# Top-k attention and two MoE layers on one core: keys and queries turned as plain numbers, scores of two heads on two halves of the array's rows, weight conversion without a drain

## The chip, the cores and the metric

The kernel runs on one core of a Trainium2 chip. Its time is the device time of one execution in microseconds; the kernel before took 2362.32 us, the median of three runs.

## The reference

Three stages follow each other. The inputs are 32-bit floats.

```python
# attention: 4 batches, 8 heads, 576 rows, head size 64
scores = scale * np.matmul(q, k.transpose(0, 1, 3, 2))
kth = np.partition(scores, -32, axis=-1)[..., -32:-31]
scores = np.where(scores >= kth, scores, -1e9)
attn = softmax(scores)                  # with 1e-9 added to the sum
x = matmul(attn, v)                     # as [2304 tokens, 512]
# first MoE: no nonlinearity, so w3 @ w_out is one matrix W
x = ((x @ w1) * (x @ w2)) @ w3 @ w_out  # 512 -> 1024 -> 512
# second MoE: 8 experts, gate by 8 rounds of row and column sums
P = exp(x @ w_gate - max); P = sinkhorn(P, 8)
out = sum(P[:, e:e+1] * (relu(x @ w1[e]) @ w2[e]) for e in range(8))
```

## The kernel before

**Numbers in two parts.** Where precision is wanted at the rate of one pass, a 32-bit number is split into a part that the array's rounded format (float32r) holds, hi, and the rest, lo. A product of two such numbers is the sum of three or four products of parts. Plain 32-bit products run on TensorE as two instructions each.

**Attention.** The 32 heads come as 16 visits, a visit being a pair of heads of one batch. The work is 72 steps: a step takes 128 query rows of both heads of a visit, and every ninth step takes the last 64 rows of two visits together. A step is a pipeline of operations with one-letter names: S0 and S1 (st_scores, the scores of head 0 and of head 1 of the next step, on TensorE, then a copy out by ScalarE and a sum of halves by GpSimd), T0 and T1 (st_top, a maximum of the score halves on VectorE), f, d, g, e (finding and dropping the eight largest of 288 numbers, VectorE, ten of them), V and J (tail and join, L299 to L306), O (st_over), E (st_exp), N, R and A (normalising, turning and multiplying the weights of the two steps before by the values). The letters F, P, C and X are where other work is put: F runs some of `fill`, P a piece of the preparation of keys and queries, C one tick of the weight conversion (convert), X takes up a finished batch. The strings in ORDERS are that order, written out by hand: one for the first ten steps, one for the rest.

**Keys and queries.** load_pair brings a visit's keys and queries. prep_split splits them in their natural layout (ScalarE rounds, GpSimd subtracts); hi and lo of one head stand side by side, 128 wide. prep_group turns nine blocks each of keys and of queries on TensorE, so hi stands on rows 0 to 63 and lo on rows 64 to 127, and ScalarE evicts them. prep_swap makes by DMA a second copy of the keys with hi and lo exchanged. A score is then two products over all 128 rows: one with the plain copy and one with the swapped copy.

**Weights.** w_out (8 tiles), w3 (16), w1 (8) and w2 (8) pass through a conversion of three ScalarE operations, one on VectorE (c1, L458) and one or two on GpSimd (cv_run, run_cv); c1 is put three slots ahead in dve_q, which every find and drop advances by one. From w3 and w_out the matrix W is made on TensorE, in `fill`, 5500 ns of it a step. NCA is the number of conversions before those of w2. When it is reached, run_cv waits until nothing is under way, frees the space of w3 and w_out (wt_close), opens that of w2 and begins again. When all is converted, moe1_pool opens the pool of the first MoE, at the earliest in step 19 (marks[0]).

**First MoE.** moe1_list gives the work of a batch in two parts of 256 and 320 tokens: ab makes the two products (12 instructions for each block of 128 outputs), x2_mm the product with W, logits the gate's products. `per` spreads the work of batches 0 to 2 evenly over the steps up to the last mark; batch 3 follows the attention. Then the second MoE runs, which the change doesn't touch.

Of the kernel before, what the change touches and what calls it, by code (L numbers as in the profile page):

```python
# [7 lines left out]
F32 = mybir.dt.float32  # L8
# [10 lines left out]
def kernel(  # L19
# [14 lines left out]
    nc = tc.nc  # L34
# [28 lines left out]
    wg = const.tile([128, KD, E], F32, name="wg")  # L63
    nc.sync.dma_start(wg, w_gate.rearrange("(c p) e -> p c e", p=128))
# [17 lines left out]
    nc.vector.tensor_scalar(ident, jp, 0.0, None, op0=ALU.is_equal)  # L82
    nc.gpsimd.memset(zf, 0.0)
# [12 lines left out]
    nat = {}  # L96
    tx = aps.tile([128, 1024], F32, name="tx")
    vn_t = [ap1.tile([128, 2 * R + 2, D], F32, name=f"vn{i}") for i in range(2)]
    qst_t = [ap1.tile([128, 2 * S4 + 256], F32R, name=f"qst{i}") for i in range(2)]
    for i in range(2):  # L100
        nc.gpsimd.memset(vn_t[i][:, 2 * R:, :], 0.0)
        nc.gpsimd.tensor_copy(qst_t[i][:, 2 * S4 + 64:2 * S4 + 192], zf)

    def load_pair(p):
        b, hp, (t0, t1), tail = visits[p]
        for nm, src, r0, r1, end in (("k", k, 0, R, True), ("q", q, t0, t1, tail)):
            t = ap1.tile([128, 2 * R + 1, D], F32, name=f"{nm}n", tag=f"{nm}n", bufs=1)
            nc.sync.dma_start(
                t[:, 0:2 * R].rearrange("p (h r) d -> p h (r d)", h=2)[:, :, D * r0:D * r1],
                src[b, 2 * hp:2 * hp + 2, 0:S4, :].rearrange("h (p r) d -> p h (r d)", r=R)[:, :, D * r0:D * r1])  # L110
            for i in range(2 if end else 0):
                nc.sync.dma_start(t[64 * i:64 * i + 64, 2 * R], src[b, 2 * hp + i, S4:S, :])
            nat[nm, p] = t
# [11 lines left out]
    split = {}  # L125
# [7 lines left out]
    def prep_split(p, nm, eng=nc.gpsimd):  # L133
        src = nat.pop((nm, p))
        hl = ap1.tile([128, 2 * R + 1, 2, D], F32R, name=f"{nm}hl", tag=f"{nm}hl")
        (t0, t1), tail = visits[p][2:]
        if nm == "k" or t1 - t0 == R:
            parts = [(src, hl[:, :, 0, :], hl[:, :, 1, :])]
        else:
            hr = hl[:, 0:2 * R].rearrange("p (h r) a d -> p h r a d", h=2)[:, :, t0:t1]  # L140
            parts = [(src[:, 0:2 * R].rearrange("p (h r) d -> p h r d", h=2)[:, :, t0:t1], hr[:, :, :, 0], hr[:, :, :, 1])]
            if tail:
                parts.append((src[:, 2 * R], hl[:, 2 * R, 0], hl[:, 2 * R, 1]))
# [3 lines left out]
        split[nm, p] = hl  # L147

    def qgroups(p):
        (t0, t1), tail = visits[p][2:]  # L150
        n = t1 - t0
# [1020 lines left out]
```

## Time and profile before

| what | value |
| --- | --- |
| median of 3 runs | 2362.32 us (2360.91 to 2363.93) |
| profiled execution | 2362.73 us, span 2360.9 us |
| TensorE (PE) busy | 2262.7 us, 96% |
| VectorE (DVE) busy | 1880.0 us, 80% |
| ScalarE (ACT) busy | 1260.2 us, 53% |
| GpSimd (POOL) busy | 1569.1 us, 66% |
| last join of the attention | 729.8 us |
| chain of work that ended last | 85% TensorE, 6% VectorE, 3% ScalarE, 3% GpSimd |

The span is the time from the first to the last instruction in the trace; the time of the same execution is 1.8 us longer. The busy shares are means over stages that have different limits. The attention with the conversion of the weights and three quarters of the first MoE takes the first 730 us, the rest of the first MoE about 100, the second MoE the rest.

### The profile page before, as it was taken

To read this page: it belongs to the slowest core of one execution; us is meant where nothing else is said; L and a number is where in the kernel's file an instruction comes from. 1 tells how busy PE (TensorE), PEld (TensorE's weight loads), DVE (VectorE), ACT (ScalarE), POOL (GpSimd) and SP (SyncE) were. 2 spreads that over 40 slices of the span, in tenths; PEclk is the share of its full clock that TensorE was granted. 3 is DMA by queue.
4 is the path that set the end of the run, shared out by engine and by line. 5 is a ranking of instruction groups with operands and counts; after the bars stand their busy time and mean duration, and the time that the engine had idled before them with its cause. 6 is when DMAs were issued, how large, how long until landed. Compare 5 with 4: busy or idle time off the path is not lost.

```text
span 2360.9 us, 39073 instructions
## 1 busy us (share of the span) xinstructions
PE 2262.7 (96%) x13155; PEld 2002.8 (85%) x13155; DVE 1880.0 (80%) x4386; ACT 1260.2 (53%) x2751; POOL 1569.1 (66%) x1726
## 2 busy tenths in 40 slices
PE   4797799999999999999999999999999999999999
PEld 3555699998998988899999988898988999999998
DVE  7999999999994378887778777777777777777776
ACT  6999788788774334443443453344434434344432
POOL 5888876776763156866666687666666666666664
PEclk7898899999999999999999999999999999999999
DMA  5433111111101022222222232222222322222221
GB/s 150 129 120 98 44 51 39 41 45 51 31 21 44 26 72 85 70 69 72 64 71 72 86 94 65 70 64 71 66 69 65 97 72 63 72 63 72 68 68 54
DMA packets 172313, 161.95 MB, mean 69 GB/s; under 512 B 21712, under 2 KB 136400, under 8 KB 172112
## 3 DMA queue, kind: packets, MB, share of 16 engines
q1 hardware_dynamic: 172112, 159.45, 22.7%
q8 instruction: 104, 1.70, 0.3%
q14 instruction: 97, 0.79, 0.1%
HBM read 140.53 MB, written 9.44 MB: 64 GB/s over the span
## 4 chain that ended last, share of the span: by engine, by line
PE 85%; DVE 6%; ACT 3%; POOL 3%; issue 1%; DMA 1%; SPq 0%; POOLq 0%; DVEq 0%; ACTq 0%
PE y L1059 33%; PE l1ps L998 29%; PE abps L582 9%; PE x2ps L600 5%; PE sps L240 3%; PE tx L383 2%; PE tx L349 2%; DVE tkv L289 2%; DVE rest L294 1%; PE pt L164 1%; DVE G L458 1%; PE tx L350 0%; DVE low L294 0%; PE lgps L620 0%; ACT s_sb L330 0%
## 5 line engine op out<-in xcount | busy, mean ns | idle before, releaser
L887 POOL TENSOR_TENSOR wal<-ws,wah 128x256 fp32r<-128x256 f32 x665 | 548.7, 833 | 475.9 <-ACT wah L886 468.3
L1072 DVE SCALAR_TENSOR_TENSOR acc<-y,P,acc 128x512 f32<-128x512 f32 x540 | 402.6, 745 | 206.3 <-PE y L1059 204.4
L886 ACT ACTIVATE wah<-ws 128x256 fp32r<-128x256 f32 x672 | 276.6, 413 | 516.5 <-PE l1ps L998 512.4
L1059 PE MATMUL y<-wbh,hh 128*128 128x512 f32 x1152 | 453.8, 394 | 5.2 <-ACT hh L1019 5.2
L1059 PE MATMUL y<-wbl,hh 128*128 128x512 f32 x1152 | 455.2, 395 | 0.0
L1059 PE MATMUL y<-wbh,hl 128*128 128x512 f32 x1152 | 451.9, 392 | 1.6 <-DVE hl L1022 1.2
L880 DVE TENSOR_TENSOR ws<-ws 128x256 f32<-128x256 f32 x384 | 326.1, 850 | 0.4 <-DMA ws<-in_moe_w_dram 0.3
L998 PE MATMUL l1ps<-xo0h,wah 128*128 128x384 f32 x896 | 302.7, 338 | 0.0
L998 PE MATMUL l1ps<-xo0l,wah 128*128 128x384 f32 x896 | 301.2, 336 | 0.0
L998 PE MATMUL l1ps<-xo0h,wal 128*128 128x384 f32 x896 | 301.0, 336 | 0.0
L1019 ACT ACTIVATE hh<-u 128x384 fp32r<-128x384 f32 x192 | 101.0, 526 | 296.8 <-DVE u L1011 296.8
L1059 PEld LDWEIGHTS y<-wbl,hh 128*128 128x128 f32 x1152 | 216.3, 188 | 49.1
L1059 PEld LDWEIGHTS y<-wbh,hh 128*128 128x128 f32 x1152 | 216.4, 188 | 32.3 <-ACT hh L1019 7.6
L1059 PEld LDWEIGHTS y<-wbh,hl 128*128 128x128 f32 x1152 | 216.6, 188 | 30.3 <-DVE hl L1022 4.9
L895 POOL TENSOR_TENSOR wbl<-ws,wbh 128x1024 fp32r<-128x1024 f32 x96 | 232.2, 2418 | 11.6 <-ACT wbh L894 0.2
L266 POOL TENSOR_TENSOR low<-s_sb 128x288 int32<-128x288 int32 x144 | 118.0, 820 | 98.6 <-ACT s_sb L244 95.0
L998 PEld LDWEIGHTS l1ps<-xo0l,wah 128*128 128x128 f32 x896 | 168.5, 188 | 17.2
L998 PEld LDWEIGHTS l1ps<-xo0h,wah 128*128 128x128 f32 x896 | 168.2, 188 | 14.4
L289 DVE MAX8 tkv<-rest 128x8 f32<-128x288 f32 x432 | 175.0, 446 | 0.0
L998 PEld LDWEIGHTS l1ps<-xo0h,wal 128*128 128x128 f32 x896 | 168.5, 188 | 0.0
L240 PE MATMUL sps<-kst,qst 128*128 128x288 f32 x640 | 133.2, 337 | 36.2 <-DVE top L273 35.0
L1011 DVE TENSOR_TENSOR u<-l1ps,u 128x384 f32<-128x384 f32 x288 | 157.2, 546 | 4.3 <-PE l1ps L998 2.5
(157 smaller groups left out, 5241.0 us busy)
## 6 DMA issues: line engine op xcount, KB each, us to landing
ws<-in_moe_w_dram SPq DMA_DIRECT2D x384, 128.0 KB, 2.3
ws<-in_moe_w_dram SPq DMA_DIRECT2D x96, 512.0 KB, 3.5
raw<-in_moe_w_dram SPq DMA_DIRECT2D x32, 512.0 KB, 3.8
kst<-kst SPq DMA_DIRECT2D x30, 288.0 KB, 4.0
xr<-x2s SPq DMA_DIRECT2D x12, 384.0 KB, 3.7
kn<-in_k_dram SPq DMA_DIRECT2D x16, 256.0 KB, 2.8
qn<-in_q_dram SPq DMA_DIRECT2D x16, 256.0 KB, 2.9
raw<-in_moe_w_out_dram SPq DMA_DIRECT2D x8, 512.0 KB, 4.2
```

The source lines that it names most:

```text
L240: nc.tensor.matmul(ps[:, e, 0:SH], lhs, kst[p, part][:, hh, SH * e:SH * e + SH], start=(n == 0), stop=(n == len(terms) - 1))
L289: nc.vector.max(vt[:, j, c:c + 8], x[:, j])
L582: nc.tensor.matmul(ps[:, 0:n], lhs[:, c, fs], rhs[:, c, 0:n], start=(c == 0 and j == 0), stop=(c == KD - 1 and j == 2))
L600: nc.tensor.matmul(ps[:, 0:n], W[:, f, 128 * c:128 * c + 128], G[:, f, 0:n], start=(f == 0), stop=(f == FC - 1))
L880: nc.vector.tensor_tensor(st[:, dst], st[:, x], st[:, y], op)
L886: nc.scalar.activation(hi, st[:, slot], AF.Copy)
L887: eng.tensor_tensor(lo, st[:, slot], hi.bitcast(F32), ALU.subtract)
L895: nc.gpsimd.tensor_tensor(lo, st, hi.bitcast(F32), ALU.subtract)
L998: nc.tensor.matmul(ps[:, 0:TH], lhs[:, c], rhs[:, slot, c], start=(k_ == 0), stop=(k_ == 3 * KH - 1))
L1011: nc.vector.tensor_tensor(t[nm], ps, t[x], ALU.add)
L1059: nc.tensor.matmul(ps, lhs[:, m, h, o:o + 128], rhs[:, m], start=(k_ == 0), stop=(k_ == 5))
L1072: nc.vector.scalar_tensor_tensor(a, ps, P[:, t, e:e + 1], a, op0=ALU.mult, op1=ALU.add)
```

## The change

- Keys and queries of both heads of a visit are loaded side by side, turned as plain numbers (five blocks each, prep_turn), and split after that (prep_parts). The two heads then stand on rows 0 to 63 and 64 to 127. There is no swapped copy.
- A score is four products of parts over 64 rows. st_scores takes one half of the keys for both heads; products of head 0 and head 1 alternate, on the two halves of the rows, into two banks. In the steps of last rows the two heads of a visit stand in blocks of a 128-row weight.
- st_sum runs after the second half, and st_top is one operation on both heads; T0 is gone.
- The conversion isn't drained before w2: its tiles live in a pool of their own, w2 in eight pairs of tiles over the space of w3 and w_out, opened by convert when W is made; scratch (cb) goes to xT. Waiting times of the conversion are shorter (1 tick for 4, 4 for 6).
- The gate's products of a part are made by gate_parts, four products side by side on 32 columns each, and summed by gate_sums with the constant `fold`.
- The start is reordered, and ORDERS has new strings, the third for steps in which the first MoE runs.

```diff
-    wg = const.tile([128, KD, E], F32, name="wg")
-    nc.sync.dma_start(wg, w_gate.rearrange("(c p) e -> p c e", p=128))
+    wg = const.tile([128, KD, 32], F32, name="wg")
+    nc.gpsimd.memset(wg, 0.0)
+    nc.sync.dma_start(wg[:, :, 0:E], w_gate.rearrange("(c p) e -> p c e", p=128))
+    fold = const.tile([128, 32], F32, name="fold")
...
-            t = ap1.tile([128, 2 * R + 1, D], F32, name=f"{nm}n", tag=f"{nm}n", bufs=1)
...
+            t = ap1.tile([128, R + 1, 2, D], F32, name=f"{nm}n", tag=f"{nm}n", bufs=1)
+            for i in range(2):
+                nc.sync.dma_start(t[:, r0:r1, i], src[b, 2 * hp + i, 0:S4, :].rearrange("(p r) d -> p r d", r=R)[:, r0:r1])
+            if end:
+                nc.sync.dma_start(t[0:SR, R], src[b, 2 * hp:2 * hp + 2, S4:S, :].rearrange("h s d -> s h d"))
...
+    def prep_turn(p, nm):
...
+        rows = src.rearrange("p r h d -> p r (h d)")
+        xt = ap1.tile([128, S], F32, name=f"{nm}t", tag=f"{nm}t", bufs=1)
+        by = scale if nm == "q" else 1.0
+        pt = mps.tile([128, 512], F32, name="pt", tag="mm")
+        for t in range(t0, t1):
+            nc.tensor.transpose(pt[:, 128 * t:128 * t + 128], rows[:, t], ident)
+        copy(xt[:, 128 * t0:128 * t1], pt[:, 128 * t0:128 * t1], None, by)
+        if tail:
+            pt = mps.tile([128, 512], F32, name="pt", tag="mm")
+            nc.tensor.transpose(pt[:, 0:SR], rows[0:SR, R], ident[0:SR, 0:SR])
+            copy(xt[:, S4:S], pt[:, 0:SR], None, by)
+        flat_x[nm, p] = xt
+
+    def prep_parts(p, nm, eng=nc.gpsimd):
+        xt = flat_x.pop((nm, p))
+        (t0, t1), tail = visits[p][2:]
+        if nm == "k":
+            kst[p] = ap1.tile([128, 2, S], F32R, name="kst", tag="kst", bufs=2)
+            parts = [(xt, kst[p][:, 0], kst[p][:, 1])]
         else:
...
+            d = qst_t[p % 2]
+            parts = [(xt[:, 128 * t0:128 * t1], d[:, 0, 128 * t0:128 * t1], d[:, 1, 128 * t0:128 * t1])]
+            for i in range(2 if tail else 0):
+                r, c = slice(64 * i, 64 * i + 64), slice(S4 + 64 * i, S4 + 64 * i + 64)
+                parts.append((xt[r, S4:S], d[r, 0, c], d[r, 1, c]))
         for x, hi, lo in parts:
             nc.scalar.activation(hi, x, AF.Copy)
             eng.tensor_tensor(lo, x, hi.bitcast(F32), ALU.subtract)
...
+    def st_scores(st, e):
         ps = aps.tile([128, 2, 512], F32, name="sps", tag="sps")
...
+        cols = slice(SH * e, SH * e + SH)
+        parts = [(a, c) for a in range(2) for c in range(2)]
+        for n, (a, c) in enumerate(parts):
+            for j in range(2):
+                p, h, t = steps1[st][j]
+                if h is None:
+                    lhs, rhs = qst_t[p % 2][:, a, S4:S4 + 128], kst[p][:, c, cols]
+                else:
+                    rows = slice(64 * h, 64 * h + 64)
+                    lhs, rhs = qst_t[p % 2][rows, a, 128 * t:128 * t + 128], kst[p][rows, c, cols]
+                nc.tensor.matmul(ps[:, j, 0:SH], lhs, rhs, start=(n == 0), stop=(n == len(parts) - 1))
...
+        nc.scalar.activation(s_sb[st][:, :, cols], ps[:, :, 0:SH], AF.Copy)
+        if e:
+            sps[st] = ps
+            st_sum(st)
...
+    def st_top(st):
+
+        top_sb[st] = ap1.tile([128, 2, SH], F32, name="top", tag="top", bufs=2)
+        nc.vector.tensor_tensor(top_sb[st], sps.pop(st)[:, :, 0:SH], s_sb[st][:, :, 0:SH], ALU.max)
...
-        cb = cv["p"].tile([128, CW], F32, name="cb", tag="cb", bufs=2)
+        cb = xT[1][:, HP - 2 + n, 0:CW]
...
-                cv_post.append((tick[0], split))
+                cv_post.append((tick[0], split, pos))
...
-                lambda: later(6, w_items(i, hf)))
+                lambda: later(4, w_items(i, hf)))
...
     def wt_close():
-        cvx.close()
         wt.close()
...
+        for c in reversed(range(KD)):
+            for hf in reversed(range(2)):
+                m1p["w2"][c, hf] = [pool.tile([128, CW], F32R, name=f"{n}{2 * c + hf}") for n in ("w2h", "w2l")]
...
+    def gate_parts(b, hf):
+        n = hf[1] - hf[0]
+        st = [x2t.pop((b, hf, c)) for c in range(KD)]
+        ps = mps.tile([128, 512], F32, name="lgps", tag="mm")
+        for c in range(KD):
+            nc.tensor.matmul(ps[32 * c:32 * c + 32, 0:n], wg[:, c], st[c][:, 0:n], start=True, stop=True,
+                             tile_position=(0, 32 * c))
+        nc.scalar.activation(st[1][:, 0:n], ps[:, 0:n], AF.Copy)
+        x2t[b, hf] = st[1]
+
+    def gate_sums(b, hf):
...
-            nc.tensor.matmul(ps[:, E * i:E * i + E], st[:, 128 * i:128 * i + 128], wg[:, c], start=True, stop=True)
+            nc.tensor.matmul(ps[:, E * i:E * i + E], st[:, 128 * i:128 * i + 128], fold[:, 0:E], start=True, stop=True)
...
+                        if f == 0 and wh + pt == 1 and gates:
+                            r.append(gates.pop(0))
...
-        if n == NCA and "w2" not in m1p:
-            if any(dve_q) or cv_post or fill or later_q or (FC - 1, 1) not in w3done:
-                return
-            wt_close()
-            for i in range(2):
-                cvs[n + i][1]()
-            return
-        if key not in raws or n - 2 in open_c1 or n - (3 if n < NCA else 2) in unsplit:
+        if n - 2 in open_c1 or n - 3 in unsplit:
             return
...
+    load_pair(0)
+    for i in range(RB):
+        cvs[i][1]()
...
+    prep_turn(0, "k")
+    prep_parts(0, "k", nc.vector)
+    prep_turn(0, "q")
+    prep_parts(0, "q", nc.vector)
     load_pair(1)
     load_v(0)
...
     st_scores(0, 0)
-    st_top(0, 0)
+    run_cv()
     st_scores(0, 1)
-    st_top(0, 1)
+    while dve_q:
+        dve_slot()
+    st_top(0)
     run_cv()
     run_cv()
...
     ORDERS = (
...
+        "X C N F f0 O0 S0 d0 P f1 d1 R0 O1 B F R1 f2 d2 f3 L F g0 C C P F P C C E0 F V e0 F E1 Q g1 S1 A C F F J T1",
+        "X P C N C O0 C O1 B f0 S0 C L d0 F f1 d1 F R0 F f2 E0 d2 f3 C E1 Q P g0 R1 C C F F V S1 e0 F g1 C C C T1 C C A F J F",
+        "C X f0 O0 O1 C C C N B L S0 F d0 P f1 F d1 f2 E0 d2 F f3 R0 E1 F C S1 Q F g0 V e0 C R1 F P g1 T1 C C F A J C C C C C",
     )
...
     def convert():
-        while cv_post and cv_post[0][0] <= tick[0] - 4:
+        if "w2" not in m1p and (FC - 1, 1) in w3done and not fill and not later_q:
+            wt_close()
+        while cv_post and cv_post[0][0] <= tick[0] - 1 and (cv_post[0][2] < NCA or "w2" in m1p):
             cv_post.pop(0)[1]()
...
-        order = ORDERS[0 if s < SWITCH else 1].split()
+        order = ORDERS[0 if s < SWITCH else 2 if "p" in m1p else 1].split()
```

## Rows read from the trace of the kernel before

**Rows 1.** Joins at L303: durations in ns, first and last start in us.

```profile
L303 DVE TENSOR_TENSOR tkv<-xm,tkv x72: 169/181/193, 29.5 to 729.8; 128x32 f32<-128x32 f32 x72
...
L303 DVE TENSOR_TENSOR tkv<-xm,tkv x1: 181/181/181, 197.0 to 197.0; 128x32 f32<-128x32 f32 x1
...
L303 DVE TENSOR_TENSOR tkv<-xm,tkv x6: 169/181/185, 185.7 to 239.3; 128x32 f32<-128x32 f32 x6
...
L303 DVE TENSOR_TENSOR tkv<-xm,tkv x1: 181/181/181, 271.2 to 271.2; 128x32 f32<-128x32 f32 x1
...
L303 DVE TENSOR_TENSOR tkv<-xm,tkv x1: 180/180/180, 284.1 to 284.1; 128x32 f32<-128x32 f32 x1
```

**Rows 2.** Stretches: engines' busy us (x instructions), PEclk, DMA share, GB/s.

```profile
130.90:197.00 66.10, 58.58 (x342) 37.29 (x342) 63.88 (x211) 65.24 (x134) 55.22 (x65) 1.00 0.34 103
197.00:274.00 77.00, 52.01 (x360) 41.39 (x358) 74.48 (x254) 68.43 (x142) 70.75 (x84) 0.80 0.28 86
...
420.00:600.00 180.00, 179.53 (x1496) 162.96 (x1495) 172.78 (x651) 143.40 (x319) 127.61 (x184) 1.00 0.16 43
```

**Rows 3.** VectorE's waits, 300 to 740 us: total, times, longest in us.

```profile
DVE top L273 <- ACT s_sb L244: 6.6, 16, 1.0
DVE lg L631 <- PE lgps L625: 4.7, 1, 4.7
DVE tkv L289 <- POOL low L278: 3.3, 7, 0.8
DVE rden L306 <- POOL rden L337: 2.4, 3, 1.1
```

**Rows 4.** Pieces of the chain that ended last: start us, us, what.

```profile
280.99 1.43 PE abps L582 x12
282.42 0.53 PE sps L240 x4
...
287.61 0.44 PE pt L164 x4
...
295.11 1.31 PE tx L371 x40
...
320.91 1.73 PE x2ps L600 x8
...
512.10 1.76 PE abps L582 x12
...
561.60 2.16 PE x2ps L600 x8
```

**Rows 5.** Timeline of TensorE's weight loads: start us, us, instruction, count.

```profile
509.93 0.54 PEld L620 LDWEIGHTS lgps<-wg,x2st 128*128 128x128 f32 x4
510.40 0.19 PEld L582 LDWEIGHTS abps<-xh,w1h 128*128 128x128 f32 x1
```

**Rows 6.** The conversions' VectorE operation at L458: least, median, most ns.

```profile
L458 DVE SCALAR_TENSOR_TENSOR G<-G,cb x40: 732/950/1623, 21.7 to 261.4; 128x512 uint16<-128x512 f32 x40
```

**Rows 7.** Timeline of the start, with idle time before an instruction and its releaser.

```profile
8.12 0.60 ACT L129 ACTIVATE kst<-pt 128x512 fp32r<-128x512 f32 x1 [2.00 <-PE pt L164]
...
16.94 0.50 PE L240 MATMUL sps<-kst,qst 128*128 128x288 f32 x2 [1.05 <-DMA kst<-kst]
```

**Rows 8.** Timeline of TensorE's products in a mixed step.

```profile
507.42 0.31 PE L582 MATMUL abps<-xh,w2l 128*128 128x320 f32 x1
507.66 1.31 PE L383 MATMUL tx<-et,vn 128*64 128x128 f32 x20
508.90 1.32 PE L240 MATMUL sps<-kst,qst 128*128 128x288 f32 x8
510.06 0.51 PE L620 MATMUL lgps<-wg,x2st 128*128 128x8 f32 x4
```

**Rows 9.** Timeline of VectorE in the same stretch: one st_top.

```profile
502.69 0.45 DVE L273 TENSOR_TENSOR top<-sps,s_sb 128x288 f32<-128x288 f32 x1
```

More of the change, by code (lines that the diff above doesn't have):

```diff
@@ L259, with st_sum @@
     low_sb, top_sb, sps, tails = {}, {}, {}, {}
[L261 to L273 removed]
+    def st_sum(st):
+        low_sb[st] = ap1.tile([128, 2, SH], F32, name="low", tag="low", bufs=2)
+        x = s_sb[st].bitcast(I32)
+        for j in range(2):
+            nc.gpsimd.tensor_tensor(low_sb[st][:, j].bitcast(I32), x[:, j, 0:SH], x[:, j, SH:S], ALU.add)
+    def st_top(st):
+        top_sb[st] = ap1.tile([128, 2, SH], F32, name="top", tag="top", bufs=2)
+        nc.vector.tensor_tensor(top_sb[st], sps.pop(st)[:, :, 0:SH], s_sb[st][:, :, 0:SH], ALU.max)
     def st_low(st):
@@ L401 @@
     cvx = ExitStack()
-    cv = {"p": cvx.enter_context(tc.tile_pool(name="cv", bufs=1, side="left")), "n": 0}
+    cv = {"p": cvx.enter_context(tc.tile_pool(name="cv", bufs=1, side="right")), "n": 0}
     w3r = {}
@@ L416, in cv_next @@
     def cv_next(pos):
-        n = pos + (RB if pos < NCA else 2)
-        if n < len(cvs) and not pos < NCA <= n:
-            cvs[n][1]()
+        if pos + RB < len(cvs):
+            cvs[pos + RB][1]()
     cv_post = []
@@ L563, in x_split @@
         for c in range(0, KD, step):
-            x = xT[b][:, c:c + step, t0:t1]
+            x = xT[b % 2][:, c:c + step, t0:t1]
             nc.scalar.activation(xh[:, c:c + step, 0:n], x, AF.Copy)
@@ L574, in ab @@
         xh, xl = xs[b, hf]
-        wh, wl = ((w1h, w1l), m1p["w2"])[which]
         if part == 0:
@@ L580, in ab @@
         for c in (2 * part, 2 * part + 1):
+            if which:
+                h, o = divmod(128 * f, CW)
+                wh, wl = [w[:, o:o + 128] for w in m1p["w2"][c, h]]
+            else:
+                wh, wl = w1h[:, c, fs], w1l[:, c, fs]
             for j, (lhs, rhs) in enumerate(((wh, xh), (wh, xl), (wl, xh))):
-                nc.tensor.matmul(ps[:, 0:n], lhs[:, c, fs], rhs[:, c, 0:n],
+                nc.tensor.matmul(ps[:, 0:n], lhs, rhs[:, c, 0:n],
                                  start=(c == 0 and j == 0), stop=(c == KD - 1 and j == 2))
@@ L745 @@
         ready[p] = max(w0 - 1, ready[p - 1] + 1) if p > 1 else -1
-        for fn in ops[:2]:
+        turns, parts = ops[::2], ops[1::2]
+        for fn in turns:
             if p > 1:
@@ L750 @@
                 fn()
-        for n, fn in enumerate(ops[2:]):
-            prep.setdefault(w0 + n * (w1 - w0 + 1) // (len(ops) - 2), []).append(fn)
+        for n, fn in enumerate(parts):
+            prep.setdefault(w0 + n * (w1 - w0 + 1) // len(parts), []).append(fn)
         if p > 1:
@@ L818 @@
                 ops[f"S{j}"] = lambda j=j: st_scores(s + 1, j)
-                ops[f"T{j}"] = lambda j=j: st_top(s + 1, j)
+            ops["T1"] = lambda: st_top(s + 1)
         if new:
```

172 lines of the change are left out of this document (25 added, 147 removed).

## The prediction

> **What bounds the kernel now.** I read the page first for the stages, then the stretches of the attention stage, then one line that runs once a step (the join at L303) to date the 72 steps, then the waits of VectorE, and last the chain and TensorE's own timeline for prices.
>
> The 72 joins run from 29.5 to 729.8 us, and the change touches nothing behind them but a few gate products; 2360.9 - 729.8 = 1631.1 us of the span are taken as they are [rows 1]. Before about step 23 the steps also carry the conversion of the weights, from there on the products of the first MoE. Joins 0 to 15 are 167.5 us apart, 11.17 us a step; join 19 comes at 239.3, join 22 at 271.2, join 23 at 284.1; the 48 steps after that take 445.7 us, 9.29 each [rows 1].
>
> In the first kind of step ScalarE (65.24 of 66.1 us) and VectorE (63.88) are both full and TensorE is not (58.58); from 197 to 274 us, while the last conversions trickle, GpSimd has 70.75 of 77 [rows 2]. In the second kind TensorE is busy 179.53 of 180 us and VectorE 172.78 [rows 2]. VectorE's waits there come to 17.0 us in four groups, and each ends with somebody who is late: score evictions, gate products, GpSimd [rows 3]. So VectorE alone would need (445.7 - 17.0) / 48 = 8.93 us a step, TensorE needs the 9.29 it gets. TensorE bounds these 48 steps, VectorE stands 4% behind it.
>
> **The change part by part.** The profiled execution took 2362.73 us with a span of 2360.9, so 1.8 lie around it; the median of the runs is 2362.32. The sum is made against 2362.73.
>
> *Conversion without a drain.* Before, run_cv refuses w2 until every queue is empty. Walking the orders through the code's guards (ticks, slots of dve_q, w3done, 5500 of fill a step) gives two conversions a step until 15, then 1, 1, 2, 1, 2, 1, 1, and the MoE pool in step 23, which is what joins 22 and 23 show (12.9 us between them, the first mixed step [rows 1]). The same walk through the new guards and orders gives two a step until step 19 and the pool in step 20, the earliest that the first mark, 19, lets it be. Three more steps thus carry MoE products.
>
> What moves: the products of batches 0 to 2. By the chain, 12 abps take 1.43 us at 256 columns and 1.76 at 320, 8 x2ps 1.73 and 2.16 [rows 4]. A batch has 192 + 192 abps and 64 + 64 x2ps instructions: 22.9 + 28.2 + 13.8 + 17.3 = 82.2 us, three batches 246.6. The old gate products load 128 columns of weights for 8 moving ones, four in 0.47 us, 0.117 each [rows 5]; 40 a batch, 14 us for three. The whole 260.6 is spread over 50.6 steps now, 5.15 a step; of 9.29 that leaves 4.14 for attention. After, it is spread over 53.6.
>
> The price of compressing: steps 16 to 19 get 8 conversions where they had 5. GpSimd was at 92% with 9 of them in seven steps [rows 2], so it may become the bound of four or five steps, at 0.5 us each: between 0 and 5 us, I take 2.5. Steps 1 to 19 also get three more of the 0.95 us VectorE ops [rows 6], 2.9 us.
>
> *Keys and queries.* A visit (a head pair, 4.5 steps) turned 18 blocks and now turns 10; four take 0.44 us [rows 4]: 8 x 0.11 / 4.5 = -0.20 us of TensorE a step. ScalarE loses two of four 512-wide evictions net of small ones (0.60 each [rows 7]): -1.2 a visit, -0.27 a step; in steps 1 to 19 ScalarE is a co-bound, so I count 0.25 there, 4.8 us, and nothing later. GpSimd's subtractions stay two large ones, with two small more a visit. The swap DMA goes; in the loop it is hidden, at the start the second head's scores wait 1.05 us for it [rows 7]. At the start wg's load now waits for a memset at the head of SP's queue, with the first keys behind it; the loads of k and q come in 256-byte pieces; three raw tiles are queued ahead of pair 1, whose turns now stand ahead of step 1's scores. Between +2 and -5 us, I take -2.
>
> *Scores.* A step has 16 products of 64 rows where it had 8 of 128 (four take 0.53, 0.132 each [rows 4]). No row here shows two halves of the array's rows at once. The nearest shows two halves of its columns: 40 value products with 64-column weights in 1.31 us, 0.033 each [rows 4], where a 128-column load takes 0.117, so an estimate of 0.058 for one of 64 columns. Both loads and products of the two halves overlap there. Bounds: full overlap leaves 1.06 us a step; loads in turn make 16 x 0.117 = 1.87; nothing overlapped makes 2.12. I take the first, with 0.06 for pairing, because the column row is the nearest. The score steps then go in and out of half-array mode twice. Going into the value products costs 507.66 - 507.42 - 0.147 = 0.09 us, coming out the next eight scores take 1.16 for 1.06, 0.10 more [rows 8]; 2 x 0.19 in 8 of 9 steps is 0.34 a step.
>
> The Trainium skill (TensorEngine Tiling (Array Packing), Key Properties) says that a change of tiling mode drains the array, which speaks against this change and gives no time; the trace agrees with 0.19 us for a round. It also reports (TensorE: Matmul & The Clock Gate, Measured speedup vs the span model) 3.07 times for four row tiles; scaled to two that is 1.54, an estimate by that page, and the sum would end near 2357. No run here shows it.
>
> *One st_top for two.* 576 elements in one op for two of 0.45 us [rows 9], placed behind both score halves; between 0 and 0.45 us saved a step, I take 0.05, about the fixed part of an op. The wait it can add: the next S0 needs sps free, so it waits for T1, and behind S0 in TensorE's queue stand the fill products. T1 is at the step's end and S0 behind some of ScalarE's work in the next, so I take none. The waits of st_top on an eviction, 6.6 us, belong to both calls [rows 3]; the mid-step T0 goes, and with it its part.
>
> *Gate.* VectorE's gate ops fall from 12 a batch to 3, about -0.05 a step, and the 4.7 us wait on a gate product goes [rows 3]. TensorE: 4 column-tiled products and two or three folds for each part, about 1.3 us for 2.3; -6 us over three batches. The new gate_sums waits for an eviction; it stands two products behind gate_parts, which cover it, except at the very end, where it has no cover and costs up to 1 us. I set this against the shorter gate of batch 3.
>
> **The sum.** Start to join 0: -2. Joins 0 to 19, 209.8 us now: 2.9 - 4.8 - 1 (st_top) + 2.5 = about 0. Joins 19 to 71, 490.5 us now: TensorE a step 4.14 - 0.20 + 0.05 + 0.34 = 4.33 plus (260.6 - 6) / 53.6 = 4.75, 9.08, less what the old 9.29 holds of idle time, which rows 2 and 3 leave at 0.05 to 0.1: about 9.0. VectorE 8.93 - 0.10 = 8.83. Two engines 2% apart, coupled in order, make 9.05 (9.0 to 9.2). 52 x 9.05 + 3.5 for the first mixed step = 474.1: -16.4. The tail: 0. Together -18, 2362.73 - 18 = 2344.7; I say 2345.
>
> **The rivals.**
> *The halves don't run at once.* For it: no row shows them; against it: the column halves do. Then a step's scores take 1.87 (loads in turn) to 2.12 us, 0.67 to 0.89 a step more over 8 of 9 steps, on the engine that is the bound: 9.72 to 9.94 us a step, 509 to 520 for 490.5. With the other terms 2379 to 2391: slower. It decides from a pair of 0.19 us on: 0.05 more than taken, times 8 pairs and 8 of 9 steps and 52, is the 18 us. The Trainium skill has a rule on its side (TensorE: Matmul & The Clock Gate, LDWEIGHTS: a load's time goes by columns, not rows, so a half-height load costs a whole one); the trace bears out the columns, and says nothing on two loads at once in rows.
> *The mixed steps stay at 9.29.* Either the halves overlap only in part (a pair of 0.17), or TensorE's turns in and out cost double, or S0 now stands at T1. Then only three steps' spread, worth 490.5 - 486.6 = 4, and the start's 2 are left: 2357, within 2352 to 2363. For it: TensorE before step 20 waits at the scores for st_top again and again, VectorE and TensorE are both nearly full.
> *The drain was worth nothing*, since steps 16 to 22 were full on VectorE anyway: this is already in the sum, which counts only the spread.
>
> **How the numbers follow.** Mainly as forecast 0.62 (2334 to 2352), steps unchanged 0.19, no overlap 0.17, the rest 0.02. A measurement tells 0.2%, 4.7 us, from no change: below 2357.6 faster, above 2367 slower. Steps unchanged is half on either side of the first bound; so faster 0.71, same 0.11, slower 0.18. The range 2334 to 2363 holds the first two cases and leaves out the third and the edges, about 0.2.
>
> **What would show it.** Score products of 64 rows in pairs that start a few ns apart, about 0.14 us from pair to pair; MoE products from about 238 us; join 19 still near 237, join 71 near 712; 9.05 us between joins after that, VectorE nearer 98% busy; no waits of a gate sum of several us. Wrong would be pairs of 0.23 us or more, joins 9.7 apart, TensorE idle before S0 with st_top as the releaser, or GpSimd at 100% in steps 16 to 19 with the joins there 12 us apart.

## The result, and the profile after

The changed kernel takes 2384.88 us (median of 4 runs, 2384.46 to 2386.25) against 2362.43 before: ratio 1.0097, interval 1.0084 to 1.011. It is slower by 22.5 us; 2345 with a range of 2334 to 2363 had been predicted. Ratios and intervals are of undisturbed executions: one of e11's ten took 5067.39 us and is left out of its ratio.

The joins again date the steps; this is the line that answers to [rows 1], all 72 of them, then single ones:

```profile
L266 DVE TENSOR_TENSOR tkv<-xm,tkv x72: 169/181/192, 25.6 to 753.0; 128x32 f32<-128x32 f32 x72
...
L266 DVE TENSOR_TENSOR tkv<-xm,tkv x5: 180/180/182, 206.8 to 254.9; 128x32 f32<-128x32 f32 x5
...
L266 DVE TENSOR_TENSOR tkv<-xm,tkv x1: 180/180/180, 297.2 to 297.2; 128x32 f32<-128x32 f32 x1
```

Join 0 comes 3.9 us sooner than before, join 15 at 206.8 for 197.0, join 19 at 254.9 for 239.3, join 23 at 297.2 for 284.1, join 71 at 753.0 for 729.8; the 1630.5 us behind it are as before (1631.1). So the loss has two places: 19.5 us between joins 0 and 19, where 0 was predicted, and 7.6 between joins 19 and 71, where a gain of 16.4 was.

The stretches that answer to [rows 2] (busy us of TensorE, weight loads, VectorE, ScalarE, GpSimd, then the granted clock): six conversion steps, the four last conversion steps, the mixed steps.

```profile
133.80:206.80 73.00, 64.41 (x405) 37.49 (x406) 64.10 (x205) 66.60 (x137) 59.93 (x73) 0.95 0.32 99
206.80:254.90 48.10, 31.45 (x200) 23.55 (x198) 42.64 (x137) 41.41 (x87) 44.59 (x53) 0.59 0.22 63
297.20:735.70 438.50, 429.08 (x3685) 364.62 (x3683) 408.37 (x1481) 332.46 (x746) 303.79 (x454) 1.00 0.10 26
```

In the first, VectorE and ScalarE do what they did before (63.88 and 65.24 us of 66.1) in 73.0 us: both now have holes. In the second GpSimd is at 93% and the joins are 12.0 us apart, as the prediction feared; the low clock there (0.59) isn't what makes these steps long, since e14 (below) has 0.75 there and takes 48.0 us for 48.1. In the third VectorE needs 408.37 / 46 = 8.88 us a step, TensorE 429.08 of 438.5. The same 46 steps before:

```profile
284.10:712.70 428.60, 427.37 (x3596) 392.21 (x3595) 412.41 (x1548) 343.08 (x762) 303.37 (x439) 1.00 0.14 39
```

The score products themselves went as forecast. TensorE's timeline after, one run of 8 half-row products with its neighbours (start us, us):

```profile
303.20 0.28 PE L540 MATMUL abps<-xh,w2l 128*128 128x256 f32 x1
303.41 0.80 PE L205 MATMUL sps<-kst,qst 64*128 64x288 f32 x8
304.15 1.13 PE L558 MATMUL x2ps<-G,W 128*128 128x256 f32 x4
```

Eight take 0.74 us from start to start. One after the other they would need 8 x 0.132 = 1.06; four pairs need 0.53. The halves overlap: the two products of a pair start 0.003 us apart and the pairs 0.133 us, the first pair excepted. The 0.21 beyond that is the turn. Before the run the step from product to product is 0.21 where 0.12 is usual in this row of products, 0.09 more.

VectorE's waits from 300 to 740 us, answering to [rows 3]:

```profile
DVE rden L269 <- POOL rden L300: 17.4, 29, 1.1
DVE lg L590 <- PE lgps L588: 5.4, 3, 3.4
DVE top L236 <- ACT s_sb L208: 2.4, 6, 0.8
DVE tkv L252 <- POOL low L241: 1.7, 5, 0.5
```

The waits on evictions are down, and two others took their place: the reciprocal in the join now waits for GpSimd's addition (Q, put behind the sums of S1 in the third order), and the gate's copy for its products.

### The profile page after: what moved, and what is told of

Read it like the earlier page. It is cut to its first block, busy times and chain, and to the rows that moved or that the text cites. A ratio compares the mean times of both kernels' runs of the same rounds, so it can differ in the third digit from the quotient of the medians.

```text
span 2383.5 us, 39559 instructions
## 1 busy us (share of the span) xinstructions
PE 2284.8 (96%) x13483; PEld 1978.2 (83%) x13483; DVE 1868.6 (78%) x4279; ACT 1252.1 (53%) x2745; POOL 1574.2 (66%) x1757
## 4 chain that ended last, share of the span: by engine, by line
PE 83%; DVE 6%; ACT 5%; POOL 4%; issue 1%; DMA 0%; SPq 0%; POOLq 0%; DVEq 0%; ACTq 0%
PE y L1011 32%; PE l1ps L950 28%; PE abps L540 9%; PE x2ps L558 5%; PE sps L205 3%; PE tx L341 2%; PE tx L312 2%; DVE tkv L252 1%; ACT s_sb L293 1%; DVE hl L974 1%; DVE rest L257 1%; PE wps L490 1%; ACT et L315 1%; PE tx L313 1%; POOL low L241 1%
## 5 line engine op out<-in xcount | busy, mean ns | idle before, releaser
L832 DVE TENSOR_TENSOR ws<-ws 128x256 f32<-128x256 f32 x384 | 319.6, 833 | 0.6 <-POOL xo0l L872 0.5
L231 POOL TENSOR_TENSOR low<-s_sb 128x288 int32<-128x288 int32 x144 | 112.2, 801 | 112.8 <-ACT s_sb L208 110.3
L205 PE MATMUL sps<-kst,qst 64*128 64x288 f32 (+1 forms) x1152 | 132.2, 335 | 27.0 <-DVE top L236 23.7
```

Of the source, the lines that this page charges most:

```text
L205: nc.tensor.matmul(ps[:, j, 0:SH], lhs, rhs, start=(n == 0), stop=(n == len(parts) - 1))
L832: nc.vector.tensor_tensor(st[:, dst], st[:, x], st[:, y], op)
```

## The experiments

Where time between joins is quoted, it comes from the joins of that kernel's trace. "Border steps" are steps 38, 39, 56, 57 and 58, in which batches 1 and 2 of the first MoE are taken up; "ordinary" are the other 41 between joins 23 and 69.

| kernel | median us | ratio, interval | joins 3-15 | 15-19 | 41 ordinary, each | 5 border steps |
| --- | --- | --- | --- | --- | --- | --- |
| before | 2362.4 | | 133.4 | 42.2 | 9.27 | 48.6 |
| after | 2384.88 | 1.0097 (1.0084-1.011) | 146.8 | 48.1 | 9.37 | 54.4 |
| e1 | 2386.06 | 1.0094 (1.0079-1.0109) | 146.8 | 48.1 | 9.30 | 56.3 |
| e2 | 2385.22 | 1.0091 (1.0075-1.0106) | 142.2 | 48.1 | 9.19 | 60.8 |
| e3 | 2386.97 | 1.01 (1.0085-1.0115) | 145.4 | 49.0 | 9.37 | 54.4 |
| e4 | 2392.88 | 1.0121 (1.0104-1.0138) | 145.2 | 48.4 | 9.67 | 51.5 |
| p1 | 2362.14 | 1.0 (0.999-1.0009) | 133.9 | 47.5 | 9.13 | 53.5 |
| p3 | 2405.18 | 1.0178 (1.0163-1.0193) | 147.9 | 48.9 | 9.67 | 51.5 |
| e5 | 2458.49 | 1.0412 (1.0395-1.043) | 159.7 | 52.7 | 10.34 | 63.6 |
| e6 | 2417.31 | 1.0229 (1.0212-1.0247) | 151.9 | 49.6 | 9.75 | 59.7 |
| e8 | 2393.5 | 1.0134 (1.0119-1.0149) | 140.4 | 43.6 | 9.70 | 50.0 |
| e9 | 2375.48 | 1.0057 (1.0042-1.0072) | 144.5 | 47.9 | 9.07 | 58.2 |
| e10 | 2354.82 | 0.9971 (0.9962-0.998) | 133.9 | 47.0 | 9.08 | 54.0 |
| e11 | 2356.2 | 0.9973 (0.9963-0.9983) | 131.6 | 42.4 | 9.29 | 46.6 |
| e12 | 2367.48 | 1.0022 (1.0011-1.0032) | 136.5 | 42.3 | 9.32 | 47.7 |
| e13 | 2393.56 | 1.0134 (1.0119-1.0149) | 147.2 | 49.2 | 9.37 | 58.6 |
| e14 | 2369.53 | 1.003 (1.0018-1.0041) | 141.7 | 48.0 | 8.95 | 61.8 |
| e15 | 2360.23 | 0.9995 (0.9985-1.0004) | 132.9 | 42.2 | 9.23 | 48.0 |

e1 and e4 are the changed kernel itself up to step 19, and have 146.8 and 145.2 us from join 3 to 15; so two traces of one program differ by 1.6 us there.

### The orders: e1, e2, e3

```diff
 # e1, third order
-... E1 F C S1 Q F g0 ...
+... E1 Q F C S1 F g0 ...
 # e2: the two orders of before without T0, the second for all steps from 10
 # e3, second order
-"X P C N C O0 C O1 B f0 ...
+"X N C C O0 C O1 P B f0 ...
```

> The changed kernel with one letter moved: in the order string of the mixed steps, Q (the small GpSimd operation on the softmax sums) stands ahead of S1 and so ahead of the sums of score halves in GpSimd's queue, as in the old strings. Theory 'order strings': VectorE's waits for that operation at the join (19 us from 270 to 760 us, and 4.5 at the last) go, the steps after join 23 fall from 9.50 to about 9.15 us, and the time is 2366 to 2374. Rival 'half-array turns': TensorE is the bound of the mixed steps with about 0.6 us of going in and out of half-array mode a step; the waits only move to another place, and the time stays within 4 us of 2385.

> The changed kernel with the two order strings of before (T0 left out, the second string for all steps from 10 on). Theory 'order strings': what was lost came from the new strings, so joins 3 to 15 are back near 11.2 us apart (12.2 in the changed kernel), the join no longer waits for GpSimd, and the time is 2345 to 2362. Rival 'the parts themselves' (split pieces of keys and queries on GpSimd, one late st_top, half-array turns): the steps stay at 12 and 9.5 us, and the time is 2375 or more.

> The changed kernel with the order string of steps 10 to 19 alone altered: N (the normalising on GpSimd that the turns of the weights wait for) stands first, ahead of P (a piece of the keys' or queries' splitting) and of the first conversion ticks. Theory 'order strings': TensorE's wait for the normalised weights (11.1 us from 134 to 270 us) and VectorE's following wait for score evictions (12.2 us) mostly go, joins 9 to 19 come 6 to 10 us closer, and the time is 2375 to 2380. Rival 'GpSimd or ScalarE is full there anyway': the waits move, and the time stays within 3 us of 2385.

None gains in all; e3 takes 2386.97 (1.01, 1.0085 to 1.0115) and changes no stretch by more than 1.4 us. e1 takes VectorE's waits for the addition away, but its waits for score evictions rise to 14.7 us in the mixed steps (2.4 in the changed kernel); e2 gives 4.6 us back in the conversion steps. Both make the ordinary steps shorter (9.30 and 9.19 for 9.37). The border steps take it back: 1.9 and 6.3 us more there. By the total alone the orders would seem not to matter; the table shows that they do.

### The two halves of the change: p1, p3, and the pool's start: e4

p1 is the kernel before with the conversion's part alone (no drain, w2 in a pool of its own, shorter waiting times); p3 is the changed kernel with that part undone. e4:

```diff
-        if s >= marks[0] and "p" not in m1p and cpos[0] == len(cvs) ...
+        if s >= 23 and "p" not in m1p and cpos[0] == len(cvs) ...
```

> The kernel before with the conversion's part of the change alone: no drain, conversion tiles in a pool of their own, w2 in eight pairs of tiles, shorter waiting times; scores, keys and queries, gate and order strings are those of before. By the code's guards the MoE pool opens in step 20. Theory 'the scores' half-array turns and the rest of the attention cost the time, the undrained conversion is good': joins 0 to 15 stay at 11.1 to 11.3 us a step, the mixed steps fall under 9.29, and the time is 2340 to 2356. Rival 'the conversion is what slows the first 20 steps' (operations queued one tick after what they wait for): joins 3 to 15 come 12 us apart as in the changed kernel, and the time is 2362 or more.

> The changed kernel with the conversion's part undone: drained before w2 and with the waiting times of before; scores, keys and queries, gate and order strings are the new ones. Theory 'the attention's part costs the time': steps 3 to 15 stay near 12 us, the MoE starts three or more steps later, and the time is 2390 to 2405. Rival 'the conversion is what slows the first 20 steps': steps 3 to 15 are back at 11.2 us and the time is 2360 to 2375.

> The changed kernel with the pool of the first MoE opened no earlier than step 23, as in the kernel before; the conversion still runs without a drain. Theory of the prediction: three steps' spread of MoE products is worth 4 to 15 us, so the time is 2389 to 2400. Rival 'the drain cost nothing that mattered, the early start collides with the last conversions': 2380 to 2386.

The conversion's part is worth nothing on the kernel before (2362.14) and 20 us on the changed one (2405.18 to 2384.88); of these the earlier pool is 8 (e4), and most of the rest the drain: joins 19 to 23 are 49.4 us apart in p3 and 39.8 in e4. The attention's part costs 43 us alone. In p1 the first batch is taken up in step 21, one later than counted (its split starts at 256.9 us, behind join 20 at 254.9). 91 fewer abps products fall in the 46 steps, 1026 for 1117, and the ordinary steps get 0.14 us shorter, 5.8 in all. The four steps to join 19 take 5.3 more and the border steps 4.9 more, which is more than that gain (the profiled execution took 2365.16 us, 3 over p1's median).

### What a turn costs: e5, e6, e8

A tiny full-array product is put into each of the 128 score runs of ordinary tiles: behind the first pair of products (e5), which makes two turns more, or behind the last (e6), which makes none; e8 puts the same product behind the runs of the kernel before.

```diff
                 nc.tensor.matmul(ps[:, j, 0:SH], lhs, rhs, start=(n == 0), stop=(n == len(parts) - 1))
+            if n == 1 and steps1[st][0][1] is not None:       # e6: n == 3
+                nc.tensor.matmul(tx[:, 704:712], ident, ident[:, 0:8], start=True, stop=True)
```

> The changed kernel with one tiny full-array product (128 rows, 8 columns, into a spare place of the turning buffer) in the middle of every run of half-array products, so that each run of eight is two runs of four: two more turns into and out of half-array mode a step in 64 of 72 steps. To be read against the next run, in which the same tiny products stand behind the runs. Theory 'TensorE is the bound and a turn costs about 0.29 us': 20 to 37 us more than the next run. Rival 'turns are covered': within 5 us of the next run.

> The changed kernel with the same tiny full-array products, but behind each run of half-array products, where full-array work follows anyway: no further turn. The products themselves take about 0.23 us each (two weight loads of 0.117), 0.4 us a step. Theory 'TensorE is the bound': 12 to 30 us more than the changed kernel, 2397 to 2415. Rival 'TensorE has room': within 5 us of 2385.

> The kernel before, with the same tiny full-array product behind each of the 128 score runs that cost the changed kernel 32 us (0.25 us each, 2385 to 2417). Theory: TensorE is the bound only in the changed kernel; before, VectorE and the handovers between the engines set the step, so the product finds room there: under 8 us, 2363 to 2371, and the steps from join 23 to 69 stay near 9.3 us. Rival, my reading before the change (TensorE bounds the 48 mixed steps): those pay in full, some 24 us, 2385 to 2395, with the mixed steps at 9.7 to 9.8 us.

e5 takes 2458.49 us (1.0412, 1.0395 to 1.043). e5 less e6 is 41.2 us for 128 rounds into and out of the half array: 0.32 us a round, where the prediction had taken 0.19 from the value products. The Trainium skill (TensorEngine Tiling (Array Packing), Key Properties) says that a change of the tiling mode drains the array; the runs agree that it costs time, and give this price. Between joins 3 and 15, where the prediction's sum has no term for the turns, the 22 added rounds cost 7.8 us (159.7 for 151.9).

e6 and e8 pay 32 and 31 us for the same 128 products, some 0.25 each. So work added to TensorE is paid in full in both kernels, and the theory that VectorE alone held the mixed steps of before falls. But it is paid between joins 3 and 15 too, 5.1 and 7.0 us for 22 products, where TensorE has idle time [rows 2]: that added work is paid doesn't yet tell that work taken out would be given back.

### One run of scores a step: e7 and its control

```diff
-    mps = mmx.enter_context(tc.tile_pool(name="mps", bufs=3, ...     # both
+    mps = mmx.enter_context(tc.tile_pool(name="mps", bufs=2, ...
-            xm = aps.tile([128, 2, TOPK // 2], F32, name="xm", tag="xm")
+            xm = tx[:, 640:640 + TOPK].rearrange("p (a b) -> p a b", a=2)
 # e7 alone: sps with bufs=2; the products of both halves at S0, the evictions where they were
```

> The changed kernel with two banks in place of three for the fill's products and the 32 values of the list's tail put into a free part of the transposes' banks: the control for the next run. Theory of the turns: neither touches the turns, 2385 to 2395. Rival (the fill's products wait for their evictions in the changed kernel): a bank less makes it worse by much more, above 2400.

> As the control, with both runs of score products of a step made one: 16 products back to back, into two pairs of banks; the evictions stay where they are. 64 steps then have one run of half products in place of two. Theory (a run of half products costs 0.32 us of TensorE for its two turns, and TensorE is the bound): 64 x 0.32 = 20 us below the control, 2365 to 2375. Rival (the turns were not it; the extra time is in the evictions of both halves, the lists' wait for them, or GpSimd): within 5 us of the control.

The control takes 2486.84 us (1.0527, 1.0509 to 1.0544), 102 more than the changed kernel. Its longest wait of VectorE isn't on a bank of the fill:

```profile
DVE tkv L266 <- PE tx L341: 84.6, 44, 5.3
```

The join now waits for value products, a wait that the changed kernel doesn't have; the edit puts the list's tail into their tile, tx. So the 102 us are of both edits together, and what the bank alone costs stays open. e7 takes 2493.88, 7 more. With so large a wait of another kind the pair says nothing on turns; it shows that the banks needed to merge the two runs aren't to be had this way.

### The changed kernel without turns: e9, and with the old orders: e14

```diff
+        if steps1[st][0][1] is not None:
+            for j in range(2):
+                p, h, t = steps1[st][j]
+                for n in range(2):
+                    nc.tensor.matmul(ps[:, j, 0:SH], qst_t[p % 2][:, n, 128 * t:128 * t + 128], kst[p][:, j, cols],
+                                     start=(n == 0), stop=(n == 1))
+            parts = []
```

> The changed kernel without its turns: in each half of an ordinary tile's scores the four pairs of half-row products (0.132 us a pair) are replaced by four products over all 128 rows and the same 288 columns, one head's bank after the other's, two products each. It leaves out half of the split terms and mixes the heads' rows, so its scores are others; work, order and columns of every engine stay. Tails keep their half products. Theory (the turns cost 0.32 us a run and TensorE is the bound): up to 128 x 0.32 = 41 us less than the changed kernel, until VectorE holds the steps as it did before: 2345 to 2355. Rival (the cost is in the shape of the evictions, the lists' start, GpSimd or the rest of the attention part): 2380 to 2387.

> Two parts undone at once: the changed kernel without turns (full-row products for the scores, as in the run that left out half of the split terms), and with the orders of the kernel before (the first head's maxima, which it no longer has, left out of them). Theory (turns and orders are separate losses in the conversion steps, 2.3 and 4.6 us from join 3 to join 15 when undone alone, and the lists' late start is 3 more of the 13.4): 139 to 141 us there in place of 146.8, the mixed steps at 9.35, and 2368 to 2373 in all. Rival (both shorten the same wait): 142 us or more there, and 2375 in all.

e9 gives back 9.4 us, far less than the 41 and far more than nothing; neither expectation held. The ordinary steps fall from 9.37 to 9.07 us, a gain of 12.0, and the border steps grow by 3.8. e14 goes on in the same way: ordinary steps of 8.95, most of them 8.8, which is VectorE's own work; border steps of 61.8. What happens in those is seen best in e14, from the end of step 55 (586.7 us) to join 56 (602.8). Stretches of 3 us:

```profile
588.00:591.00 3.00, 0.38 (x1) 0.19 (x1) 3.00 (x13) 2.20 (x4) 2.05 (x3) 1.00 0.27 67
591.00:594.00 3.00, 1.85 (x9) 1.34 (x13) 0.86 (x5) 0.00 (x0) 2.60 (x3) 0.59 0.00 0
594.00:597.00 3.00, 3.00 (x18) 2.26 (x11) 0.00 (x0) 1.01 (x3) 0.00 (x0) 0.50 0.00 0
597.00:600.00 3.00, 2.73 (x15) 2.62 (x14) 1.35 (x5) 2.10 (x6) 0.21 (x1) 0.50 0.00 0
600.00:603.00 3.00, 3.00 (x20) 2.98 (x20) 2.97 (x10) 1.53 (x4) 0.93 (x2) 0.71 0.00 0
```

and TensorE's timeline there, idle time and its releaser in brackets:

```profile
589.72 0.38 PE L547 MATMUL abps<-xh,w1h 128*128 128x256 f32 x1 [2.11 <-ACT xh L526]
592.15 0.58 PE L547 MATMUL abps<-xl,w1h 128*128 128x256 f32 x1 [2.05 <-POOL xl L527]
592.53 0.41 PE L547 MATMUL abps<-xh,w1l 128*128 128x256 f32 x1
...
593.51 1.30 PE L584 MATMUL lgps<-x2st,wg 128*32 128x320 f32 x8
```

The fill has run dry: the batch before is finished, and the first products of the new one stand in TensorE's queue behind a split that ScalarE and GpSimd only now make. TensorE idles 2.11 and 2.05 us around one product. In the second of these holes its granted clock falls from 1.00 to 0.50, the 1.2 GHz level, and stays there from 591.5 to 601.8 us; a product of 256 columns takes 0.21 from start to start for 0.12. The gate's products, which the change put between the first products of the next batch, stand behind all this, and VectorE with its list behind their copy: it does nothing from 591.9 to 598.1. The changed kernel has the same at 601 to 609 us, smaller:

```profile
601.61 0.38 PE L540 MATMUL abps<-xh,w1h 128*128 128x256 f32 x1 [0.62 <-ACT xh L519]
...
604.05 0.47 PE L540 MATMUL abps<-xl,w1h 128*128 128x256 f32 x1 [2.06 <-POOL xl L520]
...
608.39 0.17 DVE L590 COPY lg<-lgps 128x16 f32<-128x16 f32 x1 [3.37 <-PE lgps L588]
```

and so has p1, with this clock in its step 56:

```profile
586.00:588.00 2.00, 0.39 (x1) 0.19 (x1) 1.97 (x8) 0.99 (x4) 1.69 (x1) 0.85 0.04 9
588.00:590.00 2.00, 1.28 (x6) 1.28 (x7) 2.00 (x8) 0.00 (x0) 2.00 (x3) 0.50 0.00 0
```

Every kernel of the table that takes up the first batch in step 20 or 21 has 53.5 us or more in the five border steps; those that do in step 23 have 46.6 to 51.5. e4 shows it within the changed kernel: with the pool from 23 on the border steps take 51.5 for 54.4, and in both places TensorE waits for no split:

```profile
PE tx L312 <- POOL s_sb L306: 1.5, 1, 1.5
```

The early pool still gains 8 us in all there, since the ordinary steps of e4 take 9.67 for 9.37.

### Less work for VectorE: e10, e11

```diff
-                "g0": lambda: find(low, LOW), "e0": lambda: drop(low, LOW, low), ...
+                "g0": lambda: find(low, LOW), "e0": dve_slot, ...
```

> The kernel before with the conversion part alone (2362.1), less two of VectorE's list instructions per step (the drop on the lower list, 1.04 us a step, so that its next maxima repeat the first ones). Theory (there VectorE with its waits holds the mixed steps at 9.30 us and TensorE has 0.15 us of room in one): mixed steps of 9.15 us or somewhat less, 7 us or more from join 23 to 69, and something in the conversion steps: 2345 to 2355. Rival (TensorE holds them there as before): from join 23 to 69 no change, 428 us.

> The same two instructions left out of the kernel before. Theory (TensorE and VectorE both hold its mixed steps, within 0.1 us of each other): at most 5 us from join 23 to 69 (428.6 before), a smaller gain there than with the conversion part, and the same gain in the conversion steps. Rival (VectorE alone holds them): over 20 us there.

The edit takes 0.75 us a step off VectorE's busy time from join 23 to 69 in p1 (411.43 to 376.77) and 0.77 in the kernel before (412.41 to 376.98), where 1.04 had been expected. The steps there gain 1.4 us in all on p1 (427.8 to 426.4) and 1.3 on the kernel before (428.6 to 427.3). For the kernel before that is as expected; for p1 the theory (7 us or more) falls: VectorE was not what kept p1's gain. The border steps took 4.9 of its 5.8 us.

### The lists' late start: e12, e13

e12 makes, in the kernel before, the first head's sums and maxima only behind the second run of scores; e13 moves S1 ahead in the first two orders of the changed kernel.

```diff
-        st_sum(st, j)                                   # e12
+        if j:
+            st_sum(st, 0)
+            st_sum(st, 1)
-... f1 d1 T0 f2 ... S1 J T1 C A F F
+... f1 d1 f2 ... S1 J T0 T1 C A F F
-... C C E0 F V e0 F E1 Q g1 S1 A C F F J T1        # e13
+... C C S1 E0 F V e0 F E1 Q g1 A C F F J T1
```

> The kernel before with one thing of the change alone: the sums and the maxima of the first head, which it makes as soon as that head's scores are out, are put behind the second run of scores, as in the changed kernel, where both heads' lists need both runs. The first head's maxima then read both halves from the evicted copy; products and evictions stay as they are, and the first run's banks come free a little sooner. Theory (in the conversion steps the changed kernel loses its 13 us from join 3 to join 15 not to turns but to this: VectorE and GpSimd wait for the second eviction with both heads' work): from 133.4 to 140 to 147 us there, and 2370 to 2380 in all. Rival (the place of the lists' start costs nothing, and the loss comes of the plain transposes and their splits): within 3 us of 133.4 there and of 2362 in all.

> The changed kernel with the second run of scores moved ahead in the two orders of the conversion steps, in front of the exponentials and of the fill that follows them; the order of the mixed steps stays. Theory (in the conversion steps the lists start late, since the second half's eviction stands behind ScalarE's other work): from join 3 to join 15 down from 146.8 to 135 to 141 us, and 2375 to 2380 in all. Rival (the time there is lost elsewhere): 145 to 149 there, no gain in all.

e12 loses 3.1 us from join 3 to 15 and 5 in all: the late start has a price, but not 13 us, and VectorE's waits for evictions and lower lists stay small in e12 (1.7 and 1.8 us there). e13 takes 2393.56 (1.0134, 1.0119 to 1.0149), 8.7 more than the changed kernel, with 147.2 there: the wait moves from the eviction to the tail's copy, and nothing is won.

Of the 8.7, 3.9 are in step 38, whose order e13 leaves as it is. The step in the changed kernel, then in e13:

```profile
428.00:438.80 10.80, 8.09 (x68) 6.61 (x69) 9.10 (x36) 7.36 (x16) 6.44 (x8) 1.00 0.10 28
432.50:447.30 14.80, 12.01 (x66) 9.71 (x67) 9.34 (x36) 7.24 (x16) 6.45 (x8) 0.65 0.08 20
```

TensorE's waits in it are the same, 2.1 us for the split in both and three of 0.3; in e13 the granted clock fell behind the split (0.65 in the mean of the step), in the changed kernel it stayed at 1.00. So differences of 4 us in the border steps can be the clock's alone. e9's 3.8 look like this: TensorE idles 2.6 us in each of steps 38 and 56 there, for 2.7 and 3.0 in the changed kernel, but the clock is at 0.50 for 6.8 and 10.2 us, where the changed kernel has it at 0.50 in step 56 alone, for 3.4. In e14 TensorE idles longer too, 4.4 and 4.6 us.

### The gate alone: e15

The kernel before with gate_parts, gate_sums and `fold`.

> The kernel before with the new gate alone (column-tiled products and one fold in place of 4 products a tile). My step before the change: 6 us of TensorE gone, which would show in full if TensorE alone held the mixed steps: 2356 to 2358. Theory (VectorE holds them at nearly the same length): 2360 to 2363, with join 23 to join 69 within 2 us of 428.6.

From join 23 to 69 it takes 426.5 us, 2.2 less; TensorE's busy time there falls by 5.2. In all it can't be told from no change.

## Why the prediction was wrong

By its own steps.

**Right.** The halves of the rows overlap: the busy time of the score products in the 46 mixed steps is 78.19 us for 77.35. The rival "the halves don't run at once" gave 2379 to 2391 and the time fell there, but by chance: its mechanism is refuted by the timeline. The rival "the mixed steps stay at 9.29" named turns of double the cost, which came near, but its 2357 holds none of the loss before join 19. Turning the blocks costs 14.58 us for 28.00 there, -0.29 a step for -0.20. The pool opens in step 20. VectorE's work is 8.88 a step for the 8.83 predicted, and e14's ordinary steps run at that floor. One st_top for two saves 0.15 a step (34.22 us for 41.20 in 46 steps) for 0.05. The start gives 3.9 us for 2, the tail nothing.

**The turns** ("2 x 0.19 in 8 of 9 steps is 0.34 a step") were mis-sized: 0.32 a round, so 0.57 a step. In the 41 ordinary steps the changed kernel takes 0.30 more than the one without turns (e9), and there TensorE is the bound (429.08 busy and 8.9 waiting of 438.5). By the prediction's 9.05 these steps were to gain 9.0 us and they lose 4.0; the 0.23 a step by which the turns were too cheap is 9.4 of the 13.0, if it is paid in full. The turns make ordinary steps longer than before (9.37 for 9.27) although less fill is in them; p3, with the old fill as well, has 9.67.

**The spread** ("The whole 260.6 ... After, it is spread over 53.6", then "52 x 9.05") failed by itself, whatever the turns. It took three batches as one heap that can be laid evenly over all steps. A batch can't start before the attention has made it, in steps 38 and 56. By these numbers the spread takes 0.29 a step off (260.6 / 50.6 less 260.6 / 53.6), 13 us from join 23 to 69; p1, which has it without the turns and from step 21 on (0.20 a step, 9 us), gains 0.8 there (428.6 to 427.8). By the prediction's numbers a batch of (260.6 - 6) / 3 = 84.9 us at 4.75 a step is done 17.9 steps after step 20, just as the next one arrives; before, 86.9 at 5.15 from step 23 on ended two steps after. So there is nothing left to cover the split, TensorE idles and its clock falls. That costs p1 4.9 us in the border steps and the changed kernel 2.9 (54.4 for e4's 51.5); e4's border steps, with the late pool, are 2.9 over those of before. It also eats part of what makes the ordinary steps faster: in e9 and e14 the border steps take 3.8 and 7.3 more, in part by the clock alone. That the drought comes of the early pool is shown by e4; what a split made ahead of time would give wasn't tried.

**"Joins 0 to 19 ... about 0"** was 19.5. Of that, steps 16 to 19 are 5.9, which p1 shows to be the conversion's compression (5.3; predicted 2.5). From join 3 to 15 it is 13.4. Both bounds there, VectorE and ScalarE, were counted by their work, and ScalarE's was counted wrong. Joins 0 to 19 before, in the changed kernel and in p1:

```profile
29.50:239.30 209.80, 161.58 (x1000) 112.29 (x1000) 201.25 (x663) 197.32 (x403) 171.31 (x204) 0.88 0.38 116
25.60:254.90 229.30, 176.03 (x1116) 112.90 (x1116) 206.56 (x646) 201.34 (x410) 180.55 (x221) 0.85 0.30 94
29.30:244.90 215.60, 161.46 (x1000) 113.84 (x1000) 203.10 (x665) 204.78 (x416) 180.39 (x210) 0.87 0.39 118
```

The sum takes 4.8 us off ScalarE and prices the three more conversions for VectorE alone. They cost ScalarE 7.5 us (p1), and the changed attention saves it 3.4: it has 4.0 more to do. Most of the loss is not work, though: from join 3 to 15 VectorE is busy 131.85 us for 128.94, so it idles 10.5 us more. What was not counted at all are these waits between engines. VectorE's waits there (60 to 207 us) are

```profile
DVE top L236 <- ACT s_sb L208: 7.8, 6, 2.3
DVE tkv L252 <- POOL low L241: 4.5, 11, 1.1
```

and before (64 to 197 us):

```profile
DVE top L273 <- ACT s_sb L244: 2.0, 3, 1.0
DVE tkv L289 <- POOL low L278: 0.9, 2, 0.6
```

Both heads' maxima and sums now need the second eviction, but e12, where they do too, has 1.7 and 1.8; why the eviction is late isn't shown. Undone alone, the orders give 4.6 and the turns 2.3 (hardly more than the 1.6 between two traces of one program); both together 5.1; the late start added alone costs 3.1. If these added up, which no run shows, some 5 us of the 13.4 would be left: the cause of this part stays open, and the turned and split keys and queries weren't run by themselves.

**The gate** was sized right (5.2 us of TensorE for 6), but its products stand in the worst place of a border step.

**The account** from before to after, by joins: to join 0 -3.9, to 3 +0.3, to 15 +13.4, to 19 +5.9, to 23 -2.5, ordinary steps +4.0, border steps +5.9, to 71 +0.2: 23.2 at join 71 (the parts are rounded), and -0.6 behind it.

No kernel run with the whole of the reference's work is faster than the kernel before by more than can be measured.

## What to carry to other kernels

Before spreading saved work over more steps, date when each piece of it can start: a queue that runs dry at a hand-over pays the latency that it used to cover, and may then run at the low clock. Price work that is added for every engine that does it and is nearly full. Price a change of the array's shape by a run that adds such changes and nothing else, with a control, not by the nearest other change in the trace, and don't expect all of it back when they go: here 128 more cost 41.2 us, and taking 128 out gave 9.4. Where an edit gains nothing in all, compare the ordinary steps and the exceptional ones apart: e1, e2, p1 and e9 each gained in 41 steps and lost in 5.

## What the runs showed of the hardware

A round into and out of half-row products costs 0.32 us of the kernel's time (41.2 us for 128), against the 0.19 read at the column-tiled value products. Two products of 64 rows by 288 columns side by side take the time of one (four pairs within 0.74 us, a turn included). In e14 the granted clock fell from 1.00 to 0.50 in the second of two holes of 2.11 and 2.05 us and stayed at 0.50 until 601.8 us, 9.6 us of it with TensorE at work again. The same wait of 2.1 us in step 38 was followed by a fall of the clock in e13 and by none in the changed kernel, 14.8 against 10.8 us for the step.
